# First four chunks of a spectral mix: y@w_ch per chunk with a spread, or per batch from kept transposes

## The chip, the cores and the metric

The kernel runs on one core of a Trainium2 chip. The metric is device time in microseconds (us), the median of several runs. A profile of one execution goes with it; its span is a little shorter than the timed run (460.0 us against 461.8 us for the same execution), so stages are read from the profile and the outcome from the times.

A core has five engines that run side by side and wait for each other by semaphores: PE (TensorE, matrix products; its weight loads are listed apart as PEld), DVE (VectorE), ACT (ScalarE), POOL (GpSimd, which here only issues loads) and SP (SyncE, which here issues the transfers between parts of on-chip memory and the stores). Sixteen DMA engines move the data. Here all matmuls write to PSUM, and DVE or ACT carry their results on to SBUF.

## The reference

Two layers follow each other. An attention with a decaying bias gives x (8 batches, 576 positions, 512 channels). Then a spectral mix works on x; only it matters here:

```python
X = np.fft.rfft(x, axis=1)
Xr, Xi = (np.real(X[:, :n_modes]), np.imag(X[:, :n_modes]))        # n_modes = 64
Yr = np.einsum('bmd,mde->bme', Xr, w_r) - np.einsum('bmd,mde->bme', Xi, w_i)
Yi = np.einsum('bmd,mde->bme', Xr, w_i) + np.einsum('bmd,mde->bme', Xi, w_r)
Y[:, :n_modes] = Yr + 1j * Yi
y = np.fft.irfft(Y, n=S, axis=1)
u = x + y
return (u + np.maximum(u @ w_ch, 0.0)).astype(np.float32)
```

Each of the 64 modes has its own pair of 512 x 512 matrices, w_r and w_i. They are 134 MB in fp32, and each is used once. The inverse transform is linear, so u @ w_ch = x @ w_ch + irfft(Y @ w_ch). The kernel makes use of that: it multiplies the 64 modes by w_ch, and not the 576 positions of y.

## The kernel before

The sum over the input channels d is cut into four groups of 128 (NG = 4). The first three are added up while the attention runs. The fourth, g = NG - 1, comes after it, in eight chunks of eight modes (NCK = 8, MC = 8), and is the stage that the change touches. The helper `modes` makes one chunk. Its 128 result rows are (mode, real or imaginary, batch), 16 of them for each batch:

```python
    def modes(g, c, by_tile=False):

        ps = auxpool.tile([P, DM], FP32, name="yp", tag="aux")
        for cgs in (((0, 1), (2, 3)) if by_tile else ((0, 1, 2, 3),)):
            for x, cg in ((x, cg) for x in range(4) for cg in cgs):
            for x, cg in ((x, cg) for x in range(4) for cg in cgs):
                # ... c0 and cols pick 32 columns of xs, 64 elements apart
                nc.tensor.matmul(
                    ps[32 * cg : 32 * cg + 32, :],
                    cols[:, c0 : c0 + 32, m],
                    wt[(g, m // WM, ri)][:, m % WM, :],
                    start=(x == 0), stop=(x == 3),
                    tile_position=(0, 32 * cg), skip_group_check=True,
                )
        # ... for g < NG - 1 the sum goes to y_acc
        else:
            yb = spool.tile([P, DM], FP16, name="y_sb", tag="y")
            nc.vector.tensor_tensor(out=yb, in0=ps, in1=y_acc[:, c, :], op=ALU.add)
            spread(c, 0, yb)
            return yb

    def spread(c, which, rows):

        nc.sync.dma_start(out=yv[16 * c : 16 * c + 16, :, which, :], in_=rows)
```

The inverse transform, `add_y`, needs for each batch all modes on the partitions: `yv[mode, batch, which, channel]`, where which = 0 is Y and which = 1 is Y @ w_ch. `spread` brings rows (mode, batch) to that form: a transfer of 128 KB from SBUF to SBUF that SP issues. For Y @ w_ch a chunk is first transposed and then multiplied:

```python
    def y_transposed(yb):
        ps = auxpool.tile([P, DT, P], FP16, name="yt_ps", tag="aux")
        for dt in range(DT):
            nc.tensor.transpose(ps[:, dt, :], yb[:, bass.ts(dt, P)], ident16h)
        yt = spool.tile([P, DT, P], FP16, name="yt_sb", tag="yt")
        nc.scalar.copy(out=yt, in_=ps)
        return yt

    def y_times_wch(c, yt):
        vp = auxpool.tile([P, DM], FP32, name="v_ps", tag="aux")
        for dt in range(DT):
            nc.tensor.matmul(
                vp, yt[:, dt, :], wch_sb[:, dt, :], start=(dt == 0), stop=(dt == DT - 1)
            )
        vb = spool.tile([P, DM], FP16, name="v_sb", tag="v")
        nc.vector.tensor_copy(out=vb, in_=vp)
        spread(c, 1, vb)
        return vb
```

The auxiliary PSUM pool (`auxpool`, tag "aux") has two slots, shared by `modes`, the transposes and v_ps. Between these steps `work` does independent work for the positions, so that PE has something to do while weights arrive. It transposes a pair of blocks of x (x_transposed), multiplies it by w_ch (L520, into z_ps) and puts the result by (`keep`; with "e" ACT copies it and then DVE subtracts to keep the rest, with "s" ACT alone copies it). The order of the stage:

```python
    order_z = list(kept)
    TAKE = (3, 3, 1, 2, 4, 3)
    for c in range(NCK - 2):
        yb = modes(NG - 1, c)
        for x in range(TAKE[c] - 1):
            work()
        yt = y_transposed(yb)
        work()
        y_times_wch(c, yt)
    work()
    assert not order_z and not ahead
    c = NCK - 2
    yb = modes(NG - 1, c)
    x_transposed(0)
    yt = y_transposed(yb)
    x_transposed(1)
    y_times_wch(c, yt)
    for i in range(NPRE):
        x_times_wch(i, False)
```

After that come the last chunk and, for each pair of blocks, the start of u with x, `add_y` for u and for z, the ReLU and the store. `add_y` reads yv as the moving operand:

```python
    def add_y(dst, i, which, rows=slice(0, P), start=False):

        for x, (b, T) in enumerate(pairs[i]):
            for r, bb, _ in parts(b, T):
                nc.tensor.matmul(
                    dst[x][r, :], G_sb[rows, bass.ds(T * P, r.stop - r.start)],
                    yv[rows, bb, which, :], start=start, stop=True, skip_group_check=True,
                    tile_position=(0, r.start),
                )
```

All weight loads are issued by POOL in one order, long ahead; the slots they fill are freed when `modes` has used a chunk.

Of the kernel before, what the change touches and what calls it, by code (L numbers as in the profile page):

```python
# [9 lines left out]
FP32 = mybir.dt.float32  # L10
FP16 = mybir.dt.float16
# [7 lines left out]
def kernel(  # L19
# [11 lines left out]
    nc = tc.nc  # L31
    B, H, S, D = q.shape
    NM = moe_w_r.shape[0]
    DM = H * D
    P = 128
# [5 lines left out]
    DT = DM // P  # L41
# [4 lines left out]
    MC = 8  # L46
    NCK = NM // MC
# [54 lines left out]
    wch_sb = gp.tile([P, DT, DM], FP16, name="wch_sb")  # L102
    wpool = ctx.enter_context(tc.tile_pool(name="w_sb", bufs=WB))
    spool = ctx.enter_context(tc.tile_pool(name="small_sb", bufs=2))
    auxpool = ctx.enter_context(tc.tile_pool(name="aux_psum", bufs=2, space=PSUM))
# [142 lines left out]
    with tc.tile_pool(name="cum_psum", bufs=1, space=PSUM) as cpsum:  # L248
# [5 lines left out]
            out=cum, data0=spos, data1=zer, initial=0.0, op0=ALU.add, op1=ALU.add  # L254
# [16 lines left out]
        for x in range(2):  # L271
            rows = slice(NL * x, NL * x + NL)
            nc.vector.tensor_copy(
                out=cumt4[rows, :], in_=cumt_sb[rows, NK, x::2]
# [132 lines left out]
# [5 lines that stand above are left out]
                ri, par = divmod(x, 2)  # L412
                m = c * MC + 2 * cg + par
                cols = xs[g % 2].rearrange("p k r b m -> p (k r b) m")
                c0 = (48, 16)[ri] - 16 * par
# [7 lines that stand above are left out]
        if g == 0:  # L423
            nc.vector.tensor_copy(out=y_acc[:, c, :], in_=ps)
        elif g < NG - 1:
            nc.vector.tensor_tensor(out=y_acc[:, c, :], in0=ps, in1=y_acc[:, c, :], op=ALU.add)
# [9 lines that stand above are left out]
# [44 lines left out]
    finpool = ctx.enter_context(tc.tile_pool(name="fin_sb", bufs=1))  # L480
    yv = finpool.tile([P, B, 2, DM], FP16, name="yv")
# [57 lines left out]
            z1s[i] = t.bitcast(FP32).rearrange("p (x e) -> p x e", x=2)  # L539
            nc.scalar.copy(out=z1s[i], in_=zs[i])  # L540

    def y_transposed(yb):
        ps = auxpool.tile([P, DT, P], FP16, name="yt_ps", tag="aux")
        for dt in range(DT):
            nc.tensor.transpose(ps[:, dt, :], yb[:, bass.ts(dt, P)], ident16h)
        yt = spool.tile([P, DT, P], FP16, name="yt_sb", tag="yt")
        nc.scalar.copy(out=yt, in_=ps)
        return yt

# [7 lines that stand above are left out]
        nc.vector.tensor_copy(out=vb, in_=vp)  # L557
        spread(c, 1, vb)
        return vb


    ahead = []

    def work():

        if not order_z and not ahead:
            return
        if order_z:
            i = order_z.pop(0)
            x_transposed(i)  # L570
            ahead.append(i)
        if len(ahead) == 2 or not order_z:
            i = ahead.pop(0)
            keep(i)
# [69 lines left out]
    for c in range(NCK - 2):  # L644
        yb = modes(NG - 1, c)
        for x in range(TAKE[c] - 1):
            work()
        yt = y_transposed(yb)
        work()
        y_times_wch(c, yt)  # L650
    work()
    assert not order_z and not ahead
    c = NCK - 2
# [7 lines that stand above are left out]
# [3 lines left out]
    add_y(us[0], 0, 0, slice(0, GK))  # L664
    yb = modes(NG - 1, NCK - 1, by_tile=True)
    yt = y_transposed(yb)
    add_last(us[0], 0, yb)
    vb = y_times_wch(NCK - 1, yt)
    for i in range(NPRE):
        add_y(z_of(i), i, 1, slice(0, GK))  # L670
# [73 lines left out]
```

The softmax here doesn't subtract the row's maximum and nothing guards it: scores larger than these inputs give would overflow.

## Time and profile before

| | |
|---|---|
| time, median of 3 | 461.85 us (461.4 to 463.03) |
| span of the profile | 460.0 us |
| PE busy | 355.5 us, 77% |
| DVE busy | 233.0 us, 51% |
| ACT busy | 218.3 us, 47% |
| POOL busy | 182.6 us, 40% |
| chain of waits | DMA 63%, PE 26%, DVE 5%, issue 3% |
| spreads (yv<-y_sb and yv<-v_sb) | 8 and 8 transfers of 128 KB |
| weights | 512 KB a load, two loads of w_r and two of w_i per chunk |

The page of a profile gives busy time by engine, the same in 40 slices of time, the DMA queues, and the chain of work that ended last: from the last instruction back to what released it, and so on. A chain entry "DMA w_sb<-in_moe_w_i_dram" is a load of weights, from its issue to its landing, for which the next entry waited. The timeline of an engine lists its instructions in order: start, length, engine, line, operation, out<-in, shapes, how many were merged and, in brackets, how long the engine stood idle ahead of it and who ended that. A PE entry's start is well known and its end is modelled, so the pace of matmuls is read from one start to the next.

The stage of the fourth group begins at about 338 us, overlapping the end of the attention. The eight chunks start their modes at 338.68, 353.82, 363.68, 369.81, 385.34, 399.54, 411.13 and 419.74 us.

### The profile page before, as it was taken

The numbers are of one execution on the slowest core, as the hardware profiler recorded it, in microseconds if no ns is written. First come the engines' busy times: TensorE is split into PE (matmuls) and PEld (weight loads), VectorE is DVE, ScalarE is ACT, GpSimd is POOL, SyncE is SP. The second block draws the span as 40 slices with busy tenths as digits, with TensorE's granted clock in tenths as the row PEclk, the third lists the DMA queues.
The fourth block names the chain that finished last, engine by engine and source line by source line (L and its number), as shares of the span: only waits on it lengthen the run. The fifth ranks groups of instructions, "written<-read, shape, count | busy, mean of one in ns | idle before, by whom it ended". The sixth has DMA issues, their size and how long they took to land.

```text
span 460.0 us, 10252 instructions
## 1 busy us (share of the span) xinstructions
PE 355.5 (77%) x4177; PEld 218.2 (47%) x4177; DVE 233.0 (51%) x519; ACT 218.3 (47%) x375; POOL 182.6 (40%) x269
## 2 busy tenths in 40 slices
PE   1889988974667669988677788567869848988995
PEld 1456666653444446645444545445534424444442
DVE  6775666662434336644334444334436625562675
ACT  1585886554444427734444334444512302340895
POOL 6755555544445455434544434434432223100000
PEclk9997999998778779956768767777877979999999
DMA  9999999999999999999999999999999999994697
GB/s 175 200 203 203 201 201 204 202 204 204 204 202 203 203 201 203 204 204 203 202 202 205 204 204 204 204 204 204 204 210 210 211 215 210 211 212 96 228 310 297
DMA packets 110063, 95.16 MB, mean 207 GB/s; under 512 B 28544, under 2 KB 105216, under 8 KB 110016
## 3 DMA queue, kind: packets, MB, share of 16 engines
q0 software_dynamic: 98960, 81.81, 112.3%
q1 hardware_dynamic: 11056, 12.70, 9.2%
q8 instruction: 33, 0.54, 0.4%
q14 instruction: 14, 0.11, 0.1%
HBM read 164.66 MB, written 9.44 MB: 378 GB/s over the span
## 4 chain that ended last, share of the span: by engine, by line
DMA 63%; PE 26%; DVE 5%; issue 3%; POOL 1%; ACT 0%; SPq 0%; DVEq 0%; POOLq 0%; ACTq 0%
DMA w_sb<-in_moe_w_i_dram 38%; DMA w_sb<-in_moe_w_r_dram 15%; DMA q<-in_q_dram 7%; PE z_ps L520 4%; PE sc_ps L342 3%; PE sc_ps L336 2%; PE yp L416 2%; PE av_ps L371 2%; PE tr_ps L301 2%; PE z_ps L585 2%; PE u_ps L603 2%; PE u_ps L585 2%; DMA v<-in_v_dram 2%; PE z_ps L687 1%; DMA xs<-c_negm 1%
## 5 line engine op out<-in xcount | busy, mean ns | idle before, releaser
L350 ACT ACTIVATE p_sb<-sc_ps,cumt_sb 128x576 f16<-128x576 f32 (+1 forms) x256 | 142.3, 634 | 64.6 <-PE sc_ps L342 64.5
L204 POOL DMA_DIRECT2D w_sb<-in_moe_w_i_dram x60 | 45.1, 752 | 73.7 <-DMA w_sb<-in_moe_w_i_dram 32.4
L204 POOL DMA_DIRECT2D w_sb<-in_moe_w_r_dram x60 | 45.1, 752 | 71.5 <-DMA w_sb<-in_moe_w_r_dram 25.0
L204 POOL DMA_DIRECT2D v<-in_v_dram x72 | 50.7, 705 | 37.0 <-DMA w_sb<-in_moe_w_i_dram 10.2
L336 PE MATMUL sc_ps<-negm,ident 128*128 128x256 bf16 x256 | 59.4, 321 | 0.2
L301 PE MATMUL tr_ps<-ident,q 64*64 64x64 bf16 x576 | 18.5, 217 | 50.9 <-DMA q<-in_q_dram 50.8
L416 PE MATMUL yp<-w_sb,xs 128*32 128x512 bf16 x480 | 41.4, 436 | 17.5 <-DMA w_sb<-in_moe_w_i_dram 12.8
L342 PE MATMUL sc_ps<-qtB,ktB 128*128 128x512 bf16 (+2 forms) x192 | 48.1, 372 | 0.0
L304 DVE COPY qtA<-tr_ps 64x576 bf16<-64x576 bf16 x32 | 23.8, 742 | 46.3 <-PE tr_ps L301 46.3
L321 ACT ACTIVATE p<-sc_ps,cumt 128x64 f16<-128x64 f32 x32 | 10.0, 314 | 77.9 <-PE sc_ps L317 77.9
L371 PE MATMUL av_ps<-v,p_sb 128*128 128x65 f16 x1024 | 46.6, 202 | 0.0
L304 DVE COPY ktA<-tr_ps 64x576 bf16<-64x576 bf16 x32 | 24.0, 749 | 43.8 <-PE tr_ps L301 43.8
L371 PEld LDWEIGHTS <-p_sb 128*128 128x128 f16 x1024 | 41.4, 103 | 5.5 <-issue 1.9
L301 PEld LDWEIGHTS <-q 64*64 64x64 bf16 x576 | 14.6, 129 | 53.8 <-DMA q<-in_q_dram 52.8
L342 PE MATMUL sc_ps<-qtA,ktA 65*128 65x512 bf16 (+2 forms) x192 | 38.7, 313 | 0.3 <-DVE ktA L304 0.3
L520 PE MATMUL z_ps<-wch_sb,xs 128*128 128x512 f16 x144 | 36.9, 404 | 0.7 <-ACT z L540 0.7
L376 DVE TENSOR_REDUCE den<-av_ps 128x5 f32<-128x10 f32 x64 | 10.8, 169 | 49.8 <-PE av_ps L371 49.7
L416 PEld LDWEIGHTS <-xs 128*32 128x32 bf16 x512 | 21.4, 173 | 29.0 <-issue 25.8
L381 DVE TENSOR_TENSOR x_all<-av_ps,rcp 128x320 f16<-128x320 f32 x64 | 31.5, 491 | 2.2
L342 PEld LDWEIGHTS <-ktB 128*128 128x128 bf16 x192 | 24.0, 125 | 17.3 <-issue 9.0
L304 ACT COPY ktB<-tr_ps 64x576 bf16<-64x576 bf16 x32 | 20.3, 633 | 21.1 <-DVE ktA L304 20.2
L301 PE MATMUL tr_ps<-ident,k 64*64 64x64 bf16 x576 | 18.1, 215 | 13.9 <-DVE qtB L304 8.4
(90 smaller groups left out, 500.2 us busy)
## 6 DMA issues: line engine op xcount, KB each, us to landing
w_sb<-in_moe_w_r_dram POOLq DMA_DIRECT2D x60, 512.0 KB, 11.9
w_sb<-in_moe_w_i_dram POOLq DMA_DIRECT2D x60, 512.0 KB, 11.9
q<-in_q_dram POOLq DMA_DIRECT2D x32, 144.0 KB, 9.7
k<-in_k_dram POOLq DMA_DIRECT2D x32, 144.0 KB, 10.0
v<-in_v_dram POOLq DMA_DIRECT2D x72, 64.0 KB, 10.0
out_dram<-r_sb SPq DMA_DIRECT2D x16, 256.0 KB, 2.6
out_dram<-r_w SPq DMA_DIRECT2D x16, 256.0 KB, 2.5
x_all<-in_moe_w_i_dram POOLq DMA_DIRECT2D x3, 512.0 KB, 9.8
```

What stands on the lines that cost most here:

```text
L204: nc.gpsimd.dma_start(out=dst, in_=src)
L301: nc.tensor.transpose(ps[rows, r, :], src[rows, r, :], ident16[rows, rows])
L304: copy(out=dst[n % NQ][rows, :].rearrange("d (p r) -> d p r", r=R), in_=ps[rows].rearrange("d r p -> d p r"),)
L336: nc.tensor.matmul(ps[:, bass.ds(w * S, W)], ident16, negm[:, bass.ts(r, W)], start=True, stop=False, skip_group_check=True,)
L342: nc.tensor.matmul(ps[:, c0 : c0 + i1 - i0], keys[:, w, r, :], qt[:, i0:i1], start=False, stop=True, skip_group_check=True,)
L350: nc.scalar.activation(out=pt[:, poff[x] : poff[x] + S - w * W], in_=ps[:, w * S : (w + 1) * S - w * W], func=ACTF.Exp, bias=cumt_sb[:, x, ...
L371: nc.tensor.matmul(ps[:, I, r : r + NCH], lhsT, rhs, start=(i == 0), stop=(i == len(todo) - 1), skip_group_check=True,)
L376: nc.vector.tensor_reduce(out=den, in_=ps[:, :, 0 : VW : NCH], axis=mybir.AxisListType.X, op=ALU.add)
L381: nc.vector.tensor_tensor(out=x_all[:, g, b, :, D * h : D * h + D], in0=ps[:, :, 1 : NCH], in1=rcp.unsqueeze(2).to_broadcast([P, NT, D]), ...
L416: nc.tensor.matmul(ps[32 * cg : 32 * cg + 32, :], cols[:, c0 : c0 + 32, m], wt[(g, m // WM, ri)][:, m % WM, :], start=(x == 0), stop=(x == 3),
L520: nc.tensor.matmul(z[:, x, :], xts[i][:, x, dt, :], wch_sb[:, dt, :], start=(dt == 0), stop=(last and dt == DT - 1), skip_group_check=True,)
L585: nc.tensor.matmul(dst[x][r, :], G_sb[rows, bass.ds(T * P, r.stop - r.start)], yv[rows, bb, which, :], start=start, stop=True, skip_group_ ...
```

## The change

For chunks 0 to 3 the four matmuls, the copy and the spread of y@w_ch are left out. Instead, the transposes of these four chunks are kept in one tile, `yt_first`, and after chunk 3 the product is made for each batch in turn. From the kept transposes it takes as weights the 64 columns that belong to one batch (4 chunks x 16 rows, eight elements apart). So the result has the modes of that batch on its partitions, which is the form that `yv` has, and one copy by DVE puts it there. The purpose is to have yv's second half for these chunks without the four transfers. Y itself (which = 0) is spread as before, and so are both halves of chunks 4 to 7. The arithmetic stays the same.

In instructions: 16 v_ps matmuls of 128 weight columns become 32 of 64 weight columns, all of 512 moving columns; four copies of 128 x 512 become eight of 64 x 512; four spreads of 128 KB go. The 32 matmuls stand in PE's order where the four of chunk 3 stood, ahead of the modes of chunk 4. On DVE the eight copies stand together, behind the subtraction (L535) of the pair whose z is made just before. Everything else keeps its order.

```diff
--- before.py
+++ after.py
@@ -539,11 +539,16 @@
             z1s[i] = t.bitcast(FP32).rearrange("p (x e) -> p x e", x=2)
             nc.scalar.copy(out=z1s[i], in_=zs[i])
 
-    def y_transposed(yb):
+
+
+    NY = NCK // 2
+    yt_first = finpool.tile([P, DT, NY, P], FP16, name="yt_first")
+
+    def y_transposed(yb, c=NCK):
         ps = auxpool.tile([P, DT, P], FP16, name="yt_ps", tag="aux")
         for dt in range(DT):
             nc.tensor.transpose(ps[:, dt, :], yb[:, bass.ts(dt, P)], ident16h)
-        yt = spool.tile([P, DT, P], FP16, name="yt_sb", tag="yt")
+        yt = yt_first[:, :, c, :] if c < NY else spool.tile([P, DT, P], FP16, name="yt_sb", tag="yt")
         nc.scalar.copy(out=yt, in_=ps)
         return yt
 
@@ -557,6 +562,16 @@
         nc.vector.tensor_copy(out=vb, in_=vp)
         spread(c, 1, vb)
         return vb
+
+    def first_times_wch(b):
+        vp = auxpool.tile([P, DM], FP32, name="v_ps", tag="aux")
+        n = 2 * MC * NY
+        for dt in range(DT):
+            nc.tensor.matmul(
+                vp[:n], yt_first[:, dt].rearrange("p c (x b) -> p (c x) b", b=B)[:, :, b],
+                wch_sb[:, dt, :], start=(dt == 0), stop=(dt == DT - 1),
+            )
+        nc.vector.tensor_copy(out=yv[:n, b, 1, :], in_=vp[:n])
 
 
     ahead = []
@@ -645,9 +660,13 @@
         yb = modes(NG - 1, c)
         for x in range(TAKE[c] - 1):
             work()
-        yt = y_transposed(yb)
+        yt = y_transposed(yb, c)
         work()
-        y_times_wch(c, yt)
+        if c >= NY:
+            y_times_wch(c, yt)
+        elif c == NY - 1:
+            for b in range(B):
+                first_times_wch(b)
     work()
     assert not order_z and not ahead
     c = NCK - 2
```

## The prediction

> **What bounds the kernel now.** I read the page's slices first: the DMA row stands at nine tenths until slice 36 of 40, and the PE row at eight and nine tenths in the last ten slices. So two limits lie close together in the stage that the change touches (about 340 to 420 us), and a mean does not say which one ends last. The chain of waits in order of time does:
>
> ```profile
> 327.10 15.96 DMA w_sb<-in_moe_w_i_dram
> 343.10 0.49 issue
> 343.59 21.31 DMA w_sb<-in_moe_w_i_dram
> 364.94 0.49 PE yp L416 x3
> 365.43 21.67 DMA w_sb<-in_moe_w_i_dram
> 387.14 0.68 PE yp L416 x6
> 387.81 0.55 PE xt_ps L510 x8
> 388.37 1.74 PE z_ps L520 x8
> ```
>
> Columns: start, length, what. Up to 387.14 us the chain is the stream of the weights. After it no load stands in the chain any more; to the end at 460 us it is PE with short steps of DVE and ACT. So anything done by PE before 387 us is free as long as a weight wait follows it, and anything after 387 us is paid. The timeline of PE says where the change falls:
>
> ```profile
> 369.81 0.45 PE L416 MATMUL yp<-w_sb,xs 128*32 128x512 bf16 x2
> 373.58 0.69 PE L416 MATMUL yp<-w_sb,xs 128*32 128x512 bf16 x8 [3.32 <-DMA w_sb<-in_moe_w_r_dram]
> 376.89 1.10 PE L416 MATMUL yp<-w_sb,xs 128*32 128x512 bf16 x6 [2.62 <-DMA w_sb<-in_moe_w_i_dram]
> ...
> 384.38 1.03 PE L553 MATMUL v_ps<-wch_sb,yt_sb 128*128 128x512 f16 x4
> 385.34 0.90 PE L416 MATMUL yp<-w_sb,xs 128*32 128x512 bf16 x10
> 387.14 0.68 PE L416 MATMUL yp<-w_sb,xs 128*32 128x512 bf16 x6 [0.90 <-DMA w_sb<-in_moe_w_i_dram]
> 387.75 0.62 PE L510 MATMUL xt_ps<-ident16h,x_all 128*128 128x128 f16 x8
> ```
>
> The yp groups are the chunks: 369.81 to 377.93 is c=3, which loses 5.94 us to its weights, and 385.34 is c=4, which loses only 0.90. The four v_ps matmuls at 384.38 are the y@w_ch of c=3. The changed kernel puts its burst exactly there: behind the last long wait and ahead of a wait of 0.90 us. Beyond it, c=5, 6 and 7 start at 399.54, 411.13 and 419.74 us and wait for no weights. Next, the timeline of DVE around the same spot:
>
> ```profile
> 385.63 1.23 DVE L535 TENSOR_TENSOR z<-z_ps,z 128x1024 f16<-128x1024 f32 x1 [1.82 <-ACT z L534]
> 386.77 0.68 DVE L557 CAST v_sb<-v_ps 128x512 f16<-128x512 f32 x1
> 387.85 0.69 DVE L429 TENSOR_TENSOR y_sb<-yp,y_acc 128x512 f16<-128x512 f32 x1 [0.41 <-PE yp L416]
> ```
>
> The copy out of v_ps stands behind a subtraction that waits for ACT; so it starts 1.4 us after its matmuls. Last, POOL's timeline, because each weight issue waits for an earlier load to land and is thus a clock of the stream:
>
> ```profile
> 367.99 0.74 POOL L204 DMA_DIRECT2D w_sb<-in_moe_w_r_dram  x1 [1.82 <-DMA w_sb<-in_moe_w_r_dram]
> 370.51 0.74 POOL L204 DMA_DIRECT2D w_sb<-in_moe_w_i_dram  x1 [1.78 <-DMA w_sb<-in_moe_w_i_dram]
> 374.07 0.74 POOL L204 DMA_DIRECT2D w_sb<-in_moe_w_r_dram  x1 [2.82 <-PE yp L416]
> ```
>
> A step is 2.52 us where nothing else moves, and 3.56 us from 370.51 to 374.07, when the spread of v_sb issued at 370.64 us was in flight.
>
> **What the Trainium skill says.** "TensorE: Matmul & The Clock Gate", Back-to-back issue gap: a warm matmul costs its moving columns over 2.4 GHz plus 2.5 ns, 216 ns at 512, however few columns the weights have. The trace agrees: four v_ps matmuls take 0.96 us from 384.38 to the next start, and eight z matmuls 1.73 us from 388.20 to 389.93, 216 ns each. Halving the width of the weights to 64 columns therefore saves nothing. The same page, Weight-path perf modes, gives the fast weight load only to 128 columns. The trace shows 98 ns for 128 columns (yt_sb) and 108 ns for 64 (G_sb, 128x64), so narrower weights don't load faster here. "SBUF — State Buffer", Door 1 (the note on cachelines): accesses that cross to a new 16-byte line pay. The new weights are read at a step of 8 fp16, 16 bytes, so each lands in a new line. The only wide step in this trace is L416, 32 columns at 128 bytes, with a median of 168 ns a load; no load of 64 columns at 16 bytes is shown. "DMA: Bandwidth & Descriptors", Queues, rings and completion order: the engines take turns between queues, so a spread takes turns from the weights; the 3.56 us step agrees.
>
> **The change part by part.**
> (1) Removed on PE: y@w_ch of c=0, 1, 2 and 3, four matmuls each, 0.96 us per chunk. The first three (2.9 us) lie ahead of waits for weights (c=2 waits till 364.94, c=3 till 376.89) and bring nothing. The fourth lies on the path.
> (2) Added on PE, behind c=3: 8 batches x 4 matmuls x 0.216 = 6.91 us. Before, from 384.38 to the end of c=4's yp at 387.75 was 3.37 us, the 0.90 of waiting included. Now it is 6.91 plus an unbroken yp of 1.06 us (399.54 to 400.60 for c=5) = 7.97. On the path: +4.60.
> (3) Banks and DVE. The auxiliary pool has two slots. Batches 0 and 1 end 1.73 us into the burst, at 386.11 on the old clock; batch 2 needs the copy of batch 0, which DVE can only start at 386.77 behind the subtraction and ends at 387.45. With 0.05 us of signalling that is a stall of 1.4. Then PE needs 1.73 us for two batches, and a slot's turn is 0.86 + about 0.17 for the last matmul's end (1.03 less 0.86 in the row above) + 0.69 copy + 0.1 of signals = 1.82: 0.1 over, three times, +0.3. DVE gets eight copies of 0.69 for four, since 64 partitions take as long as 128; only the burst feels it. Together +1.7.
> (4) DMA: four spreads of 128 KB are gone. Twenty-two steps of POOL from 338.06 to 398.84 take 60.78 us; at 2.52 they would take 55.4. The 5.3 us are shared by nine spreads issued in that time: 0.6 us each. Three of the four removed (issued at 354.65, 365.82 and 370.64) come ahead of c=3's last weights, so these land about 1.6 us earlier (I shade 1.8, since the last was still in flight till about 376.7), and PE starts c=3 that much sooner. The fourth speeds up weights that PE no longer waits for: nothing. -1.6.
> (5) Later: everything from c=4's end to 460 us is bound by PE and moves as a block. The 0.2 us wait for c=6's spread at 419 us should go, as the weights are all in by then: -0.2.
> (6) ACT copies yt into a tile with a step between the four blocks, 0.59 us as before: 0.
> (7) Strided weights: at 168 ns or somewhat more a load stays under the 216 ns of the matmul ahead of it, so it hides. 0 in the middle, risk upward.
> Sum: 4.60 + 1.7 - 1.6 - 0.2 = +4.5, so 461.85 becomes 466.4 us, 1.0% slower.
>
> **The rivals.**
> A: the DMA stream ends last, and the burst hides in it. For it: 63% of the chain is DMA, and the last weights are issued only at 398.84. Then four spreads at 0.6 bring 2.4 us: 459.5. Against: c=5 to c=7 wait for no weights, and PE is busy 29.79 of the 32.65 us from 387.15 to 419.80. There is no hole of 6 us behind c=3.
> B: the strided weight load becomes the bound. If 64 columns cost 280 ns, the burst grows by 32 x 0.064 = 2.0: 468.5; at 400 ns by 5.9: 472. For it: L416 takes 168 ns for only half as many columns. Against: four of those are in flight at a time[...].
> C: matmuls and copies fall into lockstep. With both slots drained one after the other a batch is 0.86 + 0.17 + 0.69 + 0.1 = 1.8, the burst 14.6 instead of 6.9 + 1.7: +6, 472.5. Against: two slots, and DVE is half idle here (5.0 busy of 10 us from 380 to 390).
> D: the missing spreads give nothing because PE or POOL sets the pace of the issues: 468.0. Against: the steps of 2.52 and 3.56 us.
> E: PE arrives at c=3 with a longer idle and gets its clock back later. z after 378.75 took 3.17 us instead of 1.89, so the phase of this can move the time by about 1 us either way.
>
> **Range and chances.** The added 28 matmuls less the known waits are well held; the stall, the gain of the spreads and the clock's phase are each uncertain by about 1 us, and B leans upward. 464.0 to 468.8 should hold it 8 times in 10. Slower by over 2% means above 471.1, which needs B or C in full: 4%. Faster by over 2% means 452.6; no part comes near: 1%. Within 2%: 95%.
>
> **What would show it.** Right: the chain stays DMA up to c=3's weights, these land 1 to 2 us sooner, one block of 32 v_ps matmuls of about 8.6 us follows, and c=4 to c=7 and the whole tail stand 4 to 5 us later with no wait for weights in c=4. Step 3 is right if batch 2 waits for DVE about 1.4 us and the rest run at 0.86 to 0.91 us a batch. Step 7 is wrong if the new loads last over 216 ns and the matmuls' spacing follows them. The prediction as a whole is wrong if c=5 to c=7 start no later than before, or if weights end up in the chain after c=4.

## The result, and the profile after

| | before | changed |
|---|---|---|
| time, median | 461.95 us (461.40 to 463.03, 4 runs) | 465.54 us (464.45 to 466.44, 4 runs) |
| ratio | | 1.0074, 95% interval 1.0045 to 1.0103 |
| span of the profile | 460.0 us | 464.0 us |

The change costs 3.4 us by the ratio (2.1 to 4.8 by its interval) and 3.6 by the medians. The chain of waits of the changed kernel shows where they come in (start, length, what):

```profile
354.91 20.65 DMA w_sb<-in_moe_w_i_dram
375.60 1.10 PE yp L416 x5
376.70 0.97 PE xt_ps L510 x8
377.67 2.68 PE z_ps L520 x8
380.57 0.57 PE xt_ps L510 x16
381.14 1.85 PE z_ps L520 x8
383.01 1.02 ACT z L534
384.05 1.23 DVE z L535
385.28 0.60 DVE yv L574
385.92 5.48 PE v_ps L570 x24
391.40 1.05 PE yp L416 x15
```

The last load of the chain is now c=3's and no longer c=4's: from 375.60 us on, PE is never late for want of weights. Then, in the middle of PE's work, the chain leaves PE: ACT's copy of z, DVE's subtraction, DVE's first copy out of v_ps, and back to PE with 24 of the 32 new matmuls. The timeline of PE has the same stretch (start, length, line, shapes, count; in brackets the idle time ahead and who ended it):

```profile
368.96 0.45 PE L416 MATMUL yp<-w_sb,xs 128*32 128x512 bf16 x2
373.06 1.10 PE L416 MATMUL yp<-w_sb,xs 128*32 128x512 bf16 x8 [3.65 <-DMA w_sb<-in_moe_w_r_dram]
375.60 1.10 PE L416 MATMUL yp<-w_sb,xs 128*32 128x512 bf16 x6 [1.44 <-DMA w_sb<-in_moe_w_i_dram]
...
382.90 2.00 PE L570 MATMUL v_ps<-wch_sb,yt_first 128*64 128x512 f16 x8
385.92 5.48 PE L570 MATMUL v_ps<-wch_sb,yt_first 128*64 128x512 f16 x24 [1.02 <-DVE yv L574]
391.33 1.12 PE L416 MATMUL yp<-w_sb,xs 128*32 128x512 bf16 x16
392.38 0.62 PE L510 MATMUL xt_ps<-ident16h,x_all 128*128 128x128 f16 x8
```

The burst lasts from 382.90 to 391.33, 8.43 us. Two batches run, PE waits for DVE, six more take 5.41 us, 0.90 each. The yp of c=4 behind it runs as one block, without the wait of 0.90 us. DVE's timeline names the cause of the stall:

```profile
384.05 1.23 DVE L535 TENSOR_TENSOR z<-z_ps,z 128x1024 f16<-128x1024 f32 x1 [1.82 <-ACT z L534]
385.19 1.27 DVE L574 CAST yv<-v_ps 64x512 f16<-64x512 f32 x2
386.98 0.68 DVE L574 CAST yv<-v_ps 64x512 f16<-64x512 f32 x1 [0.52 <-PE v_ps L570]
387.84 0.68 DVE L574 CAST yv<-v_ps 64x512 f16<-64x512 f32 x1 [0.18 <-PE v_ps L570]
388.78 0.68 DVE L574 CAST yv<-v_ps 64x512 f16<-64x512 f32 x1 [0.25 <-PE v_ps L570]
```

The first two copies start only behind the subtraction. After that DVE waits for PE at each copy. The copies start 0.86 and 0.94 us apart in turn, so at every second batch PE loses some 0.08 us too.

An execution's early stages wander by a us or so, so I set the two profiles side by side from the moment at which c=0's last weights land (343.10 before, 343.92 after; the programs do not differ ahead of the transposes of c=0):

| stretch | before, us | after, us | difference |
|---|---|---|---|
| c=0's to c=3's last weights | 33.79 | 31.68 | -2.11 |
| from there to the end of c=4's yp | 10.86 | 16.78 | +5.92 |
| from there to c=7's yp | 31.99 | 31.19 | -0.80 |
| from there to the end | 40.26 | 40.43 | +0.17 |

The sum is +3.2 us; the 0.8 us that are left to the 4.0 of the spans come before the change begins.

### The profile page after: what moved, and what is told of

It reads as the page before. It is cut to its first block, busy times and chain, and to the rows that moved or that the text cites. A ratio compares the mean times of both kernels' runs of the same rounds, so it can differ in the third digit from the quotient of the medians.

```text
span 464.0 us, 10273 instructions
## 1 busy us (share of the span) xinstructions
PE 354.3 (76%) x4193; PEld 221.5 (48%) x4193; DVE 236.0 (51%) x523; ACT 218.2 (47%) x375; POOL 182.9 (39%) x269
## 4 chain that ended last, share of the span: by engine, by line
DMA 68%; PE 22%; issue 4%; POOL 3%; DVE 2%; ACT 0%; DVEq 0%; POOLq 0%; ACTq 0%
DMA w_sb<-in_moe_w_i_dram 39%; DMA w_sb<-in_moe_w_r_dram 15%; DMA q<-in_q_dram 5%; PE z_ps L520 5%; DMA y_acc<-in_moe_w_r_dram 4%; DMA v<-in_v_dram 3%; PE yp L416 2%; DMA x_all<-in_moe_w_i_dram 2%; PE z_ps L600 2%; PE u_ps L618 2%; PE u_ps L600 2%; PE z_ps L706 1%; PE sc_ps L342 1%; PE v_ps L570 1%; POOL v L204 1%
## 5 line engine op out<-in xcount | busy, mean ns | idle before, releaser
L416 PE MATMUL yp<-w_sb,xs 128*32 128x512 bf16 x480 | 39.1, 418 | 17.0 <-DMA w_sb<-in_moe_w_i_dram 11.3
L520 PE MATMUL z_ps<-wch_sb,xs 128*128 128x512 f16 x144 | 35.5, 393 | 0.0
```

What stands on the lines that cost most here:

```text
L416: nc.tensor.matmul(ps[32 * cg : 32 * cg + 32, :], cols[:, c0 : c0 + 32, m], wt[(g, m // WM, ri)][:, m % WM, :], start=(x == 0), stop=(x == 3),
L520: nc.tensor.matmul(z[:, x, :], xts[i][:, x, dt, :], wch_sb[:, dt, :], start=(dt == 0), stop=(last and dt == DT - 1), skip_group_check=True,)
```

## The experiments

Each ratio is against the kernel before on the same chip, with its 95% interval; "in us" is the ratio on 461.95. A difference between the first row and another one is uncertain by about 1.5 us either way, as the first row's own interval is that wide; so such differences are read on the traces as well.

| run | ratio | in us |
|---|---|---|
| changed kernel | 1.0074 (1.0045 to 1.0103) | +3.4 |
| packed weights (e1) | 1.0079 (1.0066 to 1.0092) | +3.6 |
| first two copies by ACT (e2) | 1.0033 (1.0019 to 1.0046) | +1.5 |
| three chunks, behind c=2 (e3) | 0.9983 (0.9966 to 1.0000) | -0.8 |
| before, four spreads left out (e4) | 0.9963 (0.9950 to 0.9976) | -1.7 |
| half the burst left out (e5) | 1.0002 (0.9991 to 1.0012) | +0.1 |
| pairs of batches (e7) | 1.0035 (1.0026 to 1.0044) | +1.6 |
| pairs of three chunks, behind c=2 (e8) | 0.9997 (0.9988 to 1.0006) | -0.1 |
| e8 and a unit of work moved (e9) | 0.9973 (0.9961 to 0.9985) | -1.2 |
| before and the unit moved (e10) | 1.0010 (0.9997 to 1.0022) | +0.5 |

My theory is that of the prediction: PE pays for the burst because it stands behind the last long wait for weights, DVE's subtraction adds a stall, and the missing spreads give a part back. The rivals are that the strided weight loads cost the time, that the weights end last anyway, and that the copies on DVE do.

### The strided weights: e1

```diff
-    yt_first = finpool.tile([P, DT, NY, P], FP16, name="yt_first")
+    yt_first = finpool.tile([P, DT, B, 2 * MC * NY], FP16, name="yt_first")
...
+            nc.scalar.copy(
+                out=yt_first[:, :, :, 2 * MC * c : 2 * MC * c + 2 * MC].rearrange("p t b x -> p t x b"),
+                in_=ps.rearrange("p t (x b) -> p t x b", b=B),
+            )
...
-                vp[:n], yt_first[:, dt].rearrange("p c (x b) -> p (c x) b", b=B)[:, :, b],
+                vp[:n], yt_first[:, dt, b, :],
```

> The changed kernel with the kept transposes stored batch by batch, so that the 64 weight columns of a batch are contiguous. Theory (the 64-column loads of 193 ns hide under matmuls of 216 ns; the burst is set by matmuls, by the 1.3 us stall on DVE and by the slots): loads fall to about 106 ns, the burst of v_ps stays at 8.4 us and the time at 465.5 us (within 0.5). Rival (the strided loads set the pace of 0.90 us a batch): the pace falls to 0.86 us and the burst by 0.3 us; with more of it hidden in the loads, by up to 1 us.

In the view of the tile yt_first (min/median/max ns), first of the changed kernel:

```profile
L570 PEld LDWEIGHTS <-yt_first x32: 192/193/217, 382.9 to 390.8; 128*64 128x64 f16 x32
```

and then of e1:

```profile
L576 PEld LDWEIGHTS <-yt_first x32: 106/108/110, 383.6 to 391.1; 128*64 128x64 f16 x32
L552 ACT COPY yt_first<-yt_ps x4: 2450/2462/2607, 350.7 to 381.1; 128x512 f16<-128x512 f16 x4
```

The step of 16 bytes costs a load of 64 columns 85 ns, and the packing takes all of it away. Still the last six batches take 386.26 to 391.67, the same 5.41 us as with strided loads. So the loads hid under matmuls of 216 ns, and the 0.90 us a batch is not theirs. The packing has a price that I had not reckoned with: ACT's copies take 2.46 us instead of 0.59, as they write two bytes at a step of 128, and PE waits 0.82 us for the last of them. The time doesn't fall.

### The stall: e2

```diff
-        nc.vector.tensor_copy(out=yv[:n, b, 1, :], in_=vp[:n])
+        (nc.scalar.copy if b < 2 else nc.vector.tensor_copy)(out=yv[:n, b, 1, :], in_=vp[:n])
```

> The changed kernel with the copies of the first two batches given to ACT, which stands idle at that point, in place of DVE, which first has to subtract. Theory (third term: the stall of 1.3 us is the subtraction ahead of the first copy): batch 2 starts about 1 us or more sooner, the burst takes 7.2 to 7.5 us instead of 8.4, and the time falls by 1.0 to 1.3 us, to about 464.4. Rival (the weights or another wait take up what is gained): the burst is shorter, but c=5 to c=7 start as before and the time stays at 465.5 us.

PE's timeline of e2:

```profile
382.06 7.32 PE L570 MATMUL v_ps<-wch_sb,yt_first 128*64 128x512 f16 x32
389.32 1.12 PE L416 MATMUL yp<-w_sb,xs 128*32 128x512 bf16 x16
```

One unbroken block of 7.26 us, 1.17 less than with the stall. The time falls by 1.9 us by the ratios; on the trace, from the landing of c=0's weights to the end of the span, it is 1.4 us less (118.66 against 120.08). The stall is the subtraction ahead of the first copy, and it is paid in full.

### The spreads by themselves: e4

The kernel before; only the transfers go, and their part of yv is zero, so their share of the output is left out.

```diff
-        spread(c, 1, vb)
+        if c >= 4:
+            spread(c, 1, vb)
```

> The kernel before with the four spreads of v_sb of chunks 0 to 3 left out (that part of yv is set to zero once, so the output lacks their share of y@w_ch); all matmuls and copies stay. It measures the fourth term by itself. Theory: c=3's weights land 1.6 to 2.1 us sooner and all that follows with them, time 459.9 to 460.4 us. Rival 1 (the stream of weights is the bound to the end): 2.4 us, 459.5 or less. Rival 2 (the pace of the weights doesn't depend on the spreads): 461.9 us.

1.7 us less (1.1 to 2.3). From c=0's to c=3's last weights it takes 31.89 us (343.55 to 375.44), where the kernel before takes 33.79 and the changed one 31.68. Three spreads fewer thus bring 1.9 to 2.1 us, 0.6 to 0.7 each, on the trace; the time agrees. The timeline of PE shows why the fourth brings nothing:

```profile
383.15 1.09 PE L416 MATMUL yp<-w_sb,xs 128*32 128x512 bf16 x10
386.06 0.68 PE L416 MATMUL yp<-w_sb,xs 128*32 128x512 bf16 x6 [1.83 <-DMA w_sb<-in_moe_w_i_dram]
417.85 1.73 PE L416 MATMUL yp<-w_sb,xs 128*32 128x512 bf16 x16
```

c=4 waits longer for its weights than before (1.83 against 0.90 us): PE gained more at c=3 than the loads had gained by c=4. Behind it c=5 and c=6 wait for none. The last line is c=7. Its 16 matmuls take 1.73 us, where they take 1.14 in the changed kernel: here the last weights come about 0.6 us late.

### Half the burst: e5

```diff
-            for b in range(B):
+            for b in range(B // 2):
                 first_times_wch(b)
```

The other four batches' part of yv is zero, so their share of the output is left out.

> The changed kernel with only four of the eight batches in the burst (16 matmuls of 64 columns, four copies); the other four batches' part of yv is set to zero once, so the output lacks their share of y@w_ch for chunks 0 to 3. Theory (each batch is paid in full, 0.86 to 0.90 us, since PE ends last after c=3): the burst falls from 8.4 to about 4.8 us and the time by 3.5 us, to about 462.0. Rival (behind c=4 the weights end last and take up most of it): it falls by 2 us or less, and c=5 to c=7 wait for weights.

The burst runs from 381.90 to 386.73, 4.83 us in place of 8.43, and the ratio falls by 0.0072, 3.3 us (3.2 on the trace, 116.90 against 120.08 from c=0's weights). Nothing takes up the gain: c=5, c=6 and c=7 start without a wait, as in the changed kernel. So four batches cost what PE spends on them, and the rival that the weights end last has no room in the changed kernel.

### The place of the burst: e3

```diff
-    NY = NCK // 2
+    NY = 3
```

> The changed kernel with three chunks in place of four: the burst of 32 matmuls (48 weight columns) stands behind c=2, ahead of the long wait for c=3's weights, and c=3 goes the old way. Theory (PE is paid only behind c=3's weights): of the burst of about 7 us some 6 fall into the wait of 5 to 6 us at c=3, and three spreads fewer bring c=3's weights 1.6 us sooner; c=4 ends 0 to 1.5 us earlier than in the kernel before, time 460.5 to 462.0 us. Rival (the extra matmuls and copies cost the same wherever they stand): about 465 us.

```profile
370.96 7.36 PE L570 MATMUL v_ps<-wch_sb,yt_first 128*48 128x512 f16 x32
378.25 1.12 PE L416 MATMUL yp<-w_sb,xs 128*32 128x512 bf16 x16
385.07 0.90 PE L416 MATMUL yp<-w_sb,xs 128*32 128x512 bf16 x10
386.58 0.68 PE L416 MATMUL yp<-w_sb,xs 128*32 128x512 bf16 x6 [0.61 <-DMA w_sb<-in_moe_w_i_dram]
420.03 0.65 PE L416 MATMUL yp<-w_sb,xs 128*32 128x512 bf16 x4 [0.56 <-DMA w_sb<-in_moe_w_i_dram]
```

and DVE's first copy:

```profile
372.10 0.68 DVE L574 CAST yv<-v_ps 48x512 f16<-48x512 f32 x1 [2.92 <-PE v_ps L570]
```

Again 32 matmuls of 512 moving columns and eight copies, now ahead of c=3 (with 48 weight columns instead of 64, and three spreads fewer instead of four). They take 7.29 us, because DVE has no subtraction to do there: it stands idle for 2.92 us until the first batch is done. c=3's yp starts behind them without any wait, and c=4 is back at its weights; so is c=7, which waits 0.56 us (the last line). The burst, moved by one chunk, makes the kernel 4.2 us faster than the changed one. It is about 0.8 us faster than the kernel before, but the interval touches no difference. It is not the work of the change that costs, but where it stands.

### Fewer matmuls: e7 and e8

Packed weights, read out of PSUM at a step and written in runs, so that 128 columns hold two batches (the diff shows the groups and their copies; the packing is done as in e1, by ACT's copy of yt, but with the step on the side of PSUM):

```diff
-            for b in range(B):
+            for b in range(0, B, 2):
                 first_times_wch(b)
...
+                vp, yt_first[:, dt, b : b + 2, :],
...
+        for h, copy in ((0, nc.vector.tensor_copy), (1, nc.scalar.copy)):
+            copy(out=yv[:n, b + h, 1, :], in_=vp[64 * h : 64 * h + n])
```

> The changed kernel, nothing left out, with two batches to a group: the kept transposes are packed batch by batch, so that 128 contiguous weight columns hold two batches; 16 matmuls in place of 32. DVE copies the first batch of a pair and ACT the second, from partitions 64 to 127 down to 0 to 63. Theory: burst about 4.7 us in place of 8.4 (3.5 of matmuls and the stall behind the subtraction), time 3.5 us below the changed kernel, 462.0. Rival: copies of two engines or the loads of 128 columns set the pace, the burst stays above 6 us and the time above 463.

The rival holds. PE's timeline of e7:

```profile
382.15 1.89 PE L576 MATMUL v_ps<-wch_sb,yt_first 128*128 128x512 f16 x8
385.88 1.89 PE L576 MATMUL v_ps<-wch_sb,yt_first 128*128 128x512 f16 x8 [1.84 <-ACT yv L581]
388.29 1.12 PE L416 MATMUL yp<-w_sb,xs 128*32 128x512 bf16 x16 [0.53 <-ACT yv L581]
```

and both engines' timeline:

```profile
384.54 1.27 DVE L581 CAST yv<-v_ps 64x512 f16<-64x512 f32 x2
385.24 1.18 ACT L581 CAST yv<-v_ps 64x512 f16<-64x512 f32 x2 [1.88 <-DVE yv L581]
```

ACT did not copy beside DVE but behind it: both read the same v_ps tile, and ACT waited until DVE was done. A slot is thus held for two copies, not one, and the burst lasts 6.14 us for 3.46 of matmuls. The gain over the changed kernel is 1.8 us by the ratios and 2.6 on the trace (117.47 against 120.08), where I had expected 3.5.

e8 puts the same pairs, of three chunks (48 of 64 columns used for each batch), behind c=2.

> Three chunks behind c=2 as in the run with three chunks, but two batches to a group (16 matmuls, packed weights, nothing left out). The burst is then only about 3.5 us in a wait of 5 to 6 us, and c=3 starts as soon as its weights land. In the run with three chunks c=3 began 2 to 3 us after that, and c=7 waited 0.56 us for its weights. Theory A (the end of the weight stream is the bound there): as with three chunks, 460.8 to 461.3 us, with a longer wait for weights in c=4 to c=7. Theory B (PE from c=3 on is still the bound): 2 us less, 459.3.

The time (461.8 on the scale of the table) is nearer to theory A than to theory B, but not for its reason. In the chain of e8 the last load is c=4's (it lands at 385.62 us), and c=5 to c=7 wait for none. PE's timeline, and then busy us of PE, PEld, DVE, ACT and POOL, the granted clock, the DMA share and GB/s by stretch:

```profile
382.70 0.69 PE L416 MATMUL yp<-w_sb,xs 128*32 128x512 bf16 x8 [1.24 <-DMA w_sb<-in_moe_w_r_dram]
385.62 1.11 PE L416 MATMUL yp<-w_sb,xs 128*32 128x512 bf16 x6 [2.24 <-DMA w_sb<-in_moe_w_i_dram]
386.66 1.03 PE L510 MATMUL xt_ps<-ident16h,x_all 128*128 128x128 f16 x8
387.49 2.57 PE L520 MATMUL z_ps<-wch_sb,xs 128*128 128x512 f16 x8
391.16 1.89 PE L520 MATMUL z_ps<-wch_sb,xs 128*128 128x512 f16 x8 [0.65 <-ACT z L540]
```

```profile
382.00:386.00 4.00, 1.06 (x12) 0.58 (x13) 1.12 (x2) 0.00 (x0) 0.74 (x1) 0.93 1.23 204
386.00:390.00 4.00, 4.00 (x24) 1.92 (x19) 1.89 (x3) 0.00 (x0) 1.07 (x2) 0.64 1.22 217
```

PE came too early for c=4, stood idle for 3.48 us in two waits, and then had a clock of 0.64: z took 2.57 us instead of 1.89. In e3, whose PE came 0.61 us early, the clock of the same stretch was 1.00. From the end of c=4's yp to c=7's it is 33.10 us in e8 (386.66 to 419.76), 31.99 in the kernel before and 31.16 in e3 (387.20 to 418.36). What the shorter burst saved was first idle. Of the 1.94 us between e8 and e3 behind that, the slower transposes and z are about 1.1, and 0.8 go with the wait of z_ps for ACT (the last line), which e3 does not have. That the idle time lowered the clock is the likely reading and not shown: in e3 the clock was 0.60 from 366 to 370 us, where PE had waited only 1.16 and 0.79 us.

### A version that beats both, and its control: e9 and e10

```diff
-    TAKE = (3, 3, 1, 2, 4, 3)
+    TAKE = (3, 3, 2, 2, 3, 3)
```

Both have this edit; e9 on top of e8, e10 on top of the kernel before.

> The run with pairs of three chunks behind c=2, with one unit of independent work (about 2.2 us of PE) moved from chunk 4 to chunk 2, nothing left out. There PE stood idle 3.5 us at c=4 and then ran with a lowered clock. Theory (the three spreads fewer were lost to PE's idle at c=3 and c=4, and PE's work behind c=4 sets the end): the moved unit fills c=3's wait, PE reaches c=7 about 2 us sooner and waits for its weights there; time 459.5 to 460.5 us, below the kernel before by 0.3% or more. Rival (the end of the weight stream sets the end already): 461.3 to 461.7 us, as the run with pairs of three chunks.

> The control: the kernel before with the same unit of work moved from chunk 4 to chunk 2 and nothing else. Theory: the unit fills part of c=3's wait of 5.9 us and PE's work behind c=4 is 2.2 us less, but all spreads are there, so the weights of c=7 end at about 420 us as before and PE waits for them: 461 to 462 us. Rival (the order of the work alone brings the gain): 459.5 to 460.5 us.

e9 is 0.27% (0.15 to 0.39) faster than the kernel before, with nothing left out; the control is not faster. In the chain of e9, the last load is c=7's:

```profile
397.17 21.93 DMA w_sb<-in_moe_w_i_dram
419.15 0.67 PE yp L416 x4
```

PE reaches c=7 at 417.82 us and waits 0.21 us for its last weights: both limits end together. In e10 the wait there is 1.48 us, till 422.21; all sixteen spreads are still in the stream. So the order of the work brings a gain only together with the fewer transfers. The moved unit went into c=3's wait and PE reached c=7 1.94 us sooner than in e8 (417.82 against 419.76), as expected; the gain of 0.27% is just short of the 0.3% that I had named. PE's idle at c=4 was not filled (3.23 us, and the clock from 386 to 390 us was 0.50). The control came out at 462.4 us on the scale of the table, a little above the 461 to 462 expected.

## Why the prediction was right

The prediction was 466.4 us, and 465.54 was measured, with the sign, the place and the main terms as stated. On the trace the sum is +3.2 us against the +4.5 predicted: the burst with its stall cost 0.4 us less, the spreads brought 0.5 more, and the stretches after c=4 brought 0.4 more. The three misses point the same way, so no large errors cancelled; the last of them was luck. Counted from c=0's weights, c=4's yp ends 3.8 us later and c=5 to c=7 start 3.0 us later, where 4 to 5 had been said.

- **The place.** It said that c=3's wait is the last long one and the burst comes behind it. The chain has c=3's load as its last one, and e3 shows the reverse: the burst one chunk earlier costs nothing.
- **Matmuls (1, 2).** 216 ns each with 64 columns as with 128: two copies behind four matmuls each start 0.86 us apart (386.98 and 387.84). The block of e2 without a stall is 7.26 us, and half the burst (e5) takes 3.3 us off the time. With the stall, predicted +6.3 up to the end of c=4's yp, measured +5.92. Removing the matmuls of c=0 to c=2 brought nothing: c=1 and c=2 now wait 1.01 and 1.11 us in their place.
- **The stall and the slots (3).** 1.4 us predicted; on the trace batch 2 starts at 385.92, 3.02 us after the first, where two batches take 1.73: 1.3. e2 takes 1.17 of it away. After it 0.90 us a batch, within the 0.86 to 0.91 predicted. e1 rules out the loads as the cause of the extra 0.04. That it is the slots' turn fits its coming at every second batch, as there are two slots, but no run tried a third slot.
- **The spreads (4).** The mechanism was right and the size too small: -1.6 predicted, -2.1 on the trace, and -1.9 in e4, where only the transfers differ. I shaded 1.8 to 1.6 for a transfer still in flight; POOL's clock of the stream shows that there was nothing to shade. Where the step was 3.56 us with the spread of v_sb in flight, it is now 2.93 us (370.62 to 373.55) with only the spread of y_sb about, 0.63 less. Three times 0.63 are the 1.9 of e4; the 0.2 us beyond it are not explained.

```profile
370.62 0.74 POOL L204 DMA_DIRECT2D w_sb<-in_moe_w_i_dram  x1 [1.85 <-DMA w_sb<-in_moe_w_i_dram]
373.55 0.74 POOL L204 DMA_DIRECT2D w_sb<-in_moe_w_r_dram  x1 [2.19 <-DMA w_sb<-in_moe_w_r_dram]
```

- **Later (5).** -0.2 predicted, -0.80 measured between c=4 and c=7, and not for the reason given. The 0.2 us wait for c=6's spread stood in the loads of PE's weights alone (first line, of PEld) and cost its matmuls nothing: from c=5's yp to c=7's it is 20.20 us before and 20.21 after. All of the 0.80 lies ahead of c=5 (11.79 us before, 10.98 after), where z_ps waits for ACT in the kernel before (second line) and not in the changed one (third line):

```profile
419.08 0.24 PEld L585 LDWEIGHTS <-G_sb 112*128 112x128 f16 x2 [0.19 <-DMA yv<-y_sb]
391.19 1.89 PE L520 MATMUL z_ps<-wch_sb,xs 128*128 128x512 f16 x8 [0.65 <-ACT z L540]
395.01 1.89 PE L520 MATMUL z_ps<-wch_sb,xs 128*128 128x512 f16 x8
```

  I overlooked that this wait could go. It returns in e8 and in no other run; why it comes and goes stays open.
- **A misreading.** The prediction has c=5 to c=7 wait for no weights. For c=7 that is not quite so. Its yp, in the kernel before and in the changed one:

```profile
419.74 1.43 PE L416 MATMUL yp<-w_sb,xs 128*32 128x512 bf16 x16
423.57 1.14 PE L416 MATMUL yp<-w_sb,xs 128*32 128x512 bf16 x16
```

  The kernel before takes 0.29 us longer. Its last load is issued at 398.84 us and takes 21.6 to land, till about 420.5, in the middle of the group; the view merges the group and shows no wait. So in the kernel before the two limits meet at c=7 already, within 0.3 us. In the changed kernel PE comes later and the weights sooner, so this does not touch the account of the change.
- **Strided loads (7).** They last 193 ns, under 216, and hide (e1). It was the nearest of the risks: only 23 ns were left.
- **The rivals.** A (the weights end last) falls with e5. B falls with e1. C (lockstep) did not happen with one copy to a slot, but did in part in e7 with two, where PE waits 1.84 and 0.53 us for ACT's copies. D falls with e4. E, the clock, took 0.2 us off here: from c=3's last weights to the start of v_ps it is 7.30 us instead of 7.49, as z takes 2.88 us instead of 3.17.

## What to carry to other kernels

When two limits lie within a per cent of each other, ask of each piece of added work which wait follows it. Ahead of a wait for a transfer 7 us of matmuls can be free (e3), and behind the last one they are paid in full (e5). A saved transfer pays only where transfers are still being waited for (e4). An engine that gets ahead may just wait longer at the next transfer, as PE did for 3.48 us in e8, and its clock can be lower behind that. A burst of small products also needs its copies free: look at what stands ahead of the first copy in the copying engine's order.

## What the runs showed of the hardware

- A weight load of 64 fp16 columns took 193 ns at a step of 16 bytes and 108 ns packed (e1). The note on cachelines in the Trainium skill's "SBUF — State Buffer", Door 1, says that each access that crosses to a new 16-byte line pays, which agrees; the same note lets a step of 8 bf16, also 16 bytes, go free, and there the measurement decides. The longer load cost no time under matmuls of 512 columns (5.41 us for six batches either way).
- ACT's copy of 128 x 512 fp16 out of PSUM took 2.46 us where it wrote two bytes at a step of 128 (e1), and 0.59 us where it read at a step of 16 bytes and wrote runs of 32 (e7).
- Copies from partitions 64 to 127 down to 0 to 63 took ACT 0.58 us for 64 x 512 (e7), as did its copies without a shift (e2).
- PE's granted clock from 386 to 390 us was 0.64 in e8, behind waits of 1.24 and 2.24 us, 0.50 in e9, behind 1.40 and 1.83, and 1.00 in e3, behind 0.61.
- A transfer of 128 KB from SBUF to SBUF held up the stream of weights by 0.6 us (1.90 us for three, e4).
